# Four small edits to start, hand-over and tail of a layer-norm, sliding-window attention and gated-FFN kernel on one TensorE-bound core

## The chip, the cores and the metric

The kernel runs on one core of a Trainium2 chip (the other cores are idle). The metric is the device time of one execution in microseconds (us). "Fast" is the undisturbed state of an execution; every run named here was in it, at a granted TensorE clock of 0.999 or 1.0. Engines: PE is TensorE's matmuls, PEld its weight loads, DVE VectorE, ACT ScalarE, POOL GpSimd, SP SyncE, which here only issues DMAs. A trailing q (SPq) is an engine's queue of issues.

## The reference, cut to what matters

```python
x  = A_x                                   # 1 x 2048 x 640, bf16
xn = layernorm(x)                          # over the 640 columns
s  = attention(xn, k_cache, v_cache, wq, wo)   # 32 heads of 192, the last 512 cached keys
g  = silu( (silu(xn @ w_gate) * (xn @ w_up)) @ w_down )   # hidden width 1536
out = x + s * g
```

There are 16 row tiles of 128 rows, in four blocks of 512. The kernel first normalises the rows and does the whole FFN block by block, then scans over 16 pairs of heads times four blocks (64 "steps") for the attention, and last forms the output tiles.

## The kernel before

Four places matter. **The start.** x comes in row tiles; gate and up weights come in two pieces each, input chunks 0 and 1 first, then chunks 2 to 4 (the "late" weights):

```python
load_x(0, nc.scalar); load_x(1, nc.scalar)
load_first(slice(0, 2))        # gate, then up: chunks 0, 1
load_first(slice(2, NC))       # gate, then up: chunks 2, 3, 4
...
load_x(2); load_x(3)
...
banks = [(f, s) for f in range(3) for s in range(2)]      # s: 0 gate, 1 up
for t in range(4):                                        # row tiles of block 0
    order = [(*fs, [c]) for c in range(NC) for fs in banks]      # 30 matmuls
    if t == 3: order = [(*fs, range(NC)) for fs in banks]
    for k, (f, s, cs) in enumerate(order):
        if k == len(order) * 4 // 5 and t < 3:            # after 24 of the 30
            ...
            ln_apply(t + 1); ready(t + 1)      # normalise; TensorE transposes, copies to xnT
            ...
        hidden_mm(first[f][s][:, rows], s, f, rows, cs)
```

(At t = 1 the statistics of tile 3 are begun before the normalising pass of tile 2.) **The hand-over to the next block.** Rows of the following block are normalised by VectorE and transposed by DMA while a block's twelve hidden chunks f run:

```python
if nx and 6 <= f < 10:
    ln_apply(4 * b + f - 2)
    ln_transpose_dma(4 * b + f - 2)
```

**The first steps of the scan.** After the products with V, the contexts are divided by their row sums, on VectorE (`by_dve`) or on ScalarE. For steps 0 and 1 the first pair of row tiles accumulates in an `mm` tile of PSUM, the second in an `sc` tile; there are two tiles of each kind, so the next user of the tile waits for the division.

```python
st["acc"] = sc_tile() if i < 2 and q2 else mm_tile()
...
divide(i, q2, acc, (0, 1) if i < 2 and q2 == 0 else ())
```

**The tail.** Eight output tiles are written through a ring of four buffers, each of which is free again when its store has landed:

```python
ob = finp.tile([P, D], bf, name="ob", bufs=4)
...
V.tensor_tensor(to, ps, like(g2[:, t, cols]), ALU.mult)
eng.tensor_tensor(like(ob[:, cols]), to, like(sacc[:, t, cols]), ALU.add)   # eng: VectorE or GpSimd
```

The softmax here doesn't subtract the row's maximum and nothing guards it: scores larger than these inputs give would overflow.

Of the kernel before, what the change touches and what calls it, by code (L numbers as in the profile page):

```python
# [15 lines left out]
def kernel(  # L16
# [14 lines left out]
    P = nc.NUM_PARTITIONS  # L31
# [3 lines left out]
    Sq, D = x2.shape  # L35
# [7 lines left out]
    NC = D // P  # L43
# [10 lines left out]
    bf = dt.bfloat16  # L54
# [111 lines left out]
    with ExitStack() as fctx:  # L166
# [14 lines left out]
        def load_x(t, eng=nc.sync):  # L181
            x_t[t] = lnx.tile([P, D], bf, name="x_t")
            eng.dma_start(out=x_t[t][:], in_=x2[t * P : (t + 1) * P, :])
# [65 lines left out]
        def ln_sqrt(t):  # L249
            mv, rstd = ln[0]  # L250
            nc.scalar.activation(
                rstd[:, t : t + 1], mv[:, t, 1:2], ACT.Sqrt, bias=eps_t[:], scale=1.0
            )

        def ln_apply(t, parts=(slice(0, D),)):
            b, ti = divmod(t, 4)
            mv, rstd = ln[b]
            xns[t] = lnx.tile([P, D], bf, name="xn", bufs=4)
            if b == 0:
                nc.vector.reciprocal(rstd[:, t : t + 1], rstd[:, t : t + 1])  # L260
            for cols in parts:
                nc.vector.tensor_scalar(
                    xns[t][:, cols], x_t[t][:, cols], mv[:, ti, 0:1], rstd[:, ti : ti + 1],
                    op0=ALU.subtract, op1=ALU.mult,
                )

        def ln_transpose_dma(t):
            nc.sync.dma_start_transpose(
                out=xnT[:, 0:NC, t * P : (t + 1) * P], in_=xns.pop(t)[:]
            )  # L270
# [69 lines left out]
        for t in range(4):  # L340
            rows = slice(t * P, (t + 1) * P)

            order = [(*fs, [c]) for c in range(NC) for fs in banks]
            if t == 3:
                order = [(*fs, range(NC)) for fs in banks]
            for k, (f, s, cs) in enumerate(order):
                if k == len(order) * 4 // 5 and t < 3:
                    if t == 1:
                        ln_stats(3, lambda: ln_apply(2))
                    else:  # L350
                        ln_apply(t + 1)
                    ready(t + 1)
                    if t == 0:
                        ln_stats(2)
                    if t < 2:
                        ln_sqrt(t + 2)
                    else:
                        nc.scalar.activation(act_t[:], one_t[:], ACT.Silu)
                hidden_mm(first[f][s][:, rows], s, f, rows, cs)
                if t == 3 and s == 1:  # L360
                    hidden_gate(0, f, *first[f])
# [5 lines left out]
        for b in range(NB):  # L367
            if b:
                hTs[b] = ffh.tile([P, NF, 512], bf, name="hT")
            nx = b + 1 < NB  # L370
            u = 0
            for f in range(NF):
                if nx and b and f == 0:
                    for t in range(4 * b + 4, 4 * b + 8):
                        load_x(t)
                if b or f >= 4:
                    ffn_hidden(b, f)
                if nx and 2 <= f < 6:
                    ln_stats(4 * b + 2 + f)
                    if f == 5:  # L380
                        ln_rstd(b + 1, 0, 4)
                if nx and 6 <= f < 10:
                    ln_apply(4 * b + f - 2)
                    ln_transpose_dma(4 * b + f - 2)

                if b >= 1 and f % 3:
                    ffn_down(b - 1, u)
                    u += 1
                if b == 2:
                    if f == 0:  # L390
                        load_k(0)
                    elif 2 <= f < 6:
                        transpose_k(0, f - 2)
                    elif f == 6:
                        load_wq(0)
                    elif 7 <= f < 10:
                        sum_k(0, f - 7)
                elif b == 3:
                    if f < 5:
                        centre_k(0, f)  # L400
                    elif f < 8:
                        (load_k, load_wq, load_wo)[f - 5]((1, 1, 0)[f - 5])
# [12 lines left out]
    finp = ctx.enter_context(tc.tile_pool(name="fin", bufs=2))  # L415
# [5 lines left out]
    Ps, OTs, Obs, xrs = {}, {}, {}, {}  # L421
# [34 lines left out]
    def pv(i, q2):  # L456

        pr, b = divmod(i, NB)
        st = {}

        def part(p):
            if p == 0:
                if q2 == 0:
                    Obs[i] = opool.tile([P, 4, 2, Dh], bf, name="O_b")
                    tag = "OT_l" if late(i) and pr < last else "OT_b"
                    OTs[i] = otpool.tile([P, 12, P], bf, name=tag, tag=tag, bufs=2 if tag == "OT_l" else 3)
                st["acc"] = sc_tile() if i < 2 and q2 else mm_tile()
            acc = st["acc"]
            turn, h = divmod(p, 2)
            for kc in range(KC):  # L470
                for n, r in enumerate((lo, hi)):
                    k = n ^ turn
                    qt = 2 * q2 + k
                    m = nc.tensor.matmul(  # L474
                        acc[:, k, h * 256 : h * 256 + Dh + 1],
                        Ps[i][kc][r, h, qt * P : (qt + 1) * P], V_p[r, kc, h, 0 : Dh + 1],
                        start=(p == 0 and kc == 0), stop=(turn == 1 and kc == KC - 1),
                        skip_group_check=True,
                    )
                    after(m, st)  # L480
            if p == 1:
                turned(m, st)
            if p == 3:
                divide(i, q2, acc, (0, 1) if i < 2 and q2 == 0 else ())

        return [lambda p=p: part(p) for p in range(4)]

    def divide(i, q2, acc, by_dve):
        pr, b = divmod(i, NB)
        O_b, OT_b = Obs[i], OTs[i]  # L490
        r = smpool.tile([P, 2, 2, 1], f32, name="r")
        a_v = acc[:, :, :].rearrange("p k (h c) -> p k h c", h=2)
        nc.vector.reciprocal(r[:], a_v[:, :, :, Dh : Dh + 1])  # L493
        for k in range(2):
            qt = 2 * q2 + k
            a_k = a_v[:, k, :, :]
            if by_dve and k in by_dve:
                nc.vector.tensor_tensor(
                    O_b[:, qt, :, :], a_k[:, :, 0:Dh], r[:, k, :, :].to_broadcast([P, 2, Dh]),
                    ALU.mult,  # L500
                )
                continue
            for h in range(2):
                nc.scalar.activation(  # L504
                    O_b[:, qt, h, :], a_k[:, h, 0:Dh], ACT.Copy, scale=r[:, k, h, :]
                )
        nc.sync.dma_start_transpose(
            out=OT_b[:, 6 * q2 : 6 * q2 + 6, :],
            in_=O_b[:, 2 * q2 : 2 * q2 + 2, :, :].rearrange("p t h d -> p (t h d)"),
        )  # L510
# [121 lines left out]

    def wo_last(b, qt, eng):
        i, t = last * NB + b, 4 * b + qt
        ob = xrs[t] if b < 2 else finp.tile([P, D], bf, name="ob", bufs=4)
        s_f = finp.tile([P, D], f32, name="s_f", bufs=4)
        sc = mm_tile() if b == 2 and qt % 2 == 0 else sc_tile()
        for n, cols in enumerate(HALVES):
            if late(i):
                wo_cols(sc[:, n, 0:HD], i - NB, qt, cols, end=False)  # L640
            wo_cols(sc[:, n, 0:HD], i, qt, cols, first=not late(i))
        finish(sc[:, :, 0:HD], t, slice(0, D), ob, s_f, eng)
        stores.append((t, ob))

    def wo_parts(qt, parts):


        i, t, c0 = NS - 1, 4 * (NB - 1) + qt, 0
        ob = finp.tile([P, D], bf, name="ob", bufs=4)
        s_f = finp.tile([P, D], f32, name="s_f", bufs=4)  # L650
        for n, (width, eng, queue) in enumerate(parts):
            cols, c0 = slice(c0, c0 + width), c0 + width
            ps = (sc_tile() if n else mm_tile())[:, 0, 0:width]
            wo_cols(ps, i - NB, qt, cols, end=False)
            wo_cols(ps, i, qt, cols, first=False)
            finish(ps, t, cols, ob, s_f, eng)
            if queue:
                queue.dma_start(out=out2[t * P : (t + 1) * P, cols], in_=ob[:, cols])
        if not queue:
            stores.append((t, ob))  # L660
# [25 lines left out]
    for pr in range(NPAIR):  # L686
        for b in range(NB):
            i = pr * NB + b
# [22 lines left out]
        for b in range(NB):  # L711
            i = pr * NB + b
# [17 lines left out]
    i = last * NB  # L730
# [47 lines left out]
```

## Time and profile before

| | kernel before |
|---|---|
| time, the first three runs | 922.9 us median (922.84 to 922.93) |
| span of the profiled execution | 921.8 us (timed at 923.55 us, 0.65 above that median) |
| TensorE / VectorE / ScalarE / GpSimd busy | 914.4 / 576.0 / 474.0 / 101.5 us |
| first matmul starts / last one ends | 1.23 / 917.83 us |

The page of the profile cuts the span into 40 slices of 23 us; a digit is the busy share in tenths.

```profile
PE   8999999999999999999999999999999999999998
DVE  6443331467676767676666667676767676767656
ACT  4222223547464656555556565655555555556461
```

TensorE is at 9 in every slice but the first and the last: no other engine can be the bound, and whatever the change can win lies in the first slice, in the last, and in stalls too short to change a digit. That is why one has to go to the timeline.

### The profile page before, as it was taken

The numbers are of one execution on the slowest core, as the hardware profiler recorded it, in microseconds if no ns is written. First come the engines' busy times: TensorE is split into PE (matmuls) and PEld (weight loads), VectorE is DVE, ScalarE is ACT, GpSimd is POOL, SyncE is SP. The second block draws the span as 40 slices with busy tenths as digits, with TensorE's granted clock in tenths as the row PEclk, the third lists the DMA queues.
The fourth block names the chain that finished last, engine by engine and source line by source line (L and its number), as shares of the span: only waits on it lengthen the run. The fifth ranks groups of instructions, "written<-read, shape, count | busy, mean of one in ns | idle before, by whom it ended". The sixth has DMA issues, their size and how long they took to land.

```text
span 921.8 us, 25768 instructions
## 1 busy us (share of the span) xinstructions
PE 914.4 (99%) x11086; PEld 625.7 (68%) x11102; DVE 576.0 (62%) x847; ACT 474.0 (51%) x850; POOL 101.5 (11%) x390
## 2 busy tenths in 40 slices
PE   8999999999999999999999999999999999999998
PEld 5455555575858585868686767676777777776666
DVE  6443331467676767676666667676767676767656
ACT  4222223547464656555556565655555555556461
POOL 0000000000000000000000000000000000002978
PEclk9999999999999999999999999999999999999999
DMA  9312510044544444444536262635271817163524
GB/s 309 62 22 70 101 45 1 1 74 92 91 76 83 83 81 86 73 93 63 103 58 108 56 112 53 113 47 120 43 123 36 130 37 129 29 128 86 134 58 141
DMA packets 243762, 77.18 MB, mean 84 GB/s; under 512 B 224576, under 2 KB 243648, under 8 KB 243648
## 3 DMA queue, kind: packets, MB, share of 16 engines
q1 hardware_dynamic: 243216, 75.14, 41.6%
q8 instruction: 87, 1.43, 0.7%
q10 hardware_dynamic: 432, 0.39, 0.2%
q14 instruction: 27, 0.22, 0.1%
HBM read 39.45 MB, written 2.62 MB: 46 GB/s over the span
## 4 chain that ended last, share of the span: by engine, by line
PE 98%; DMA 1%; POOL 0%; DVE 0%; issue 0%; SPq 0%; POOLq 0%; DVEq 0%
PE mm L435 22%; PE sc L571 19%; PE sc L449 18%; PE mm L474 16%; PE sc L277 11%; PE mm L299 6%; PE sc L543 2%; PE mm L526 2%; DMA wu_sb<-in_B_w_up_dram 1%; PE gu L277 0%; DMA out_dram<-ob 0%; PE mm L543 0%; PE mm L312 0%; PE sc L474 0%; PE sc L526 0%; POOL ob L631 0%
## 5 line engine op out<-in xcount | busy, mean ns | idle before, releaser
L453 ACT ACTIVATE p_t<-sc 128x1024 bf16<-128x1024 f32 x254 | 252.9, 1022 | 128.4 <-PE sc L449 128.4
L440 DVE TENSOR_REDUCE qT<-mm 128x512 bf16<-128x1024 f32 x189 | 231.1, 1223 | 95.2 <-PE mm L435 92.8
L504 ACT ACTIVATE O_b<-mm,r 128x192 bf16<-128x192 f32 x482 | 163.2, 421 | 178.8 <-issue 156.3
L435 PE MATMUL mm<-xnT,wq_p 64*128 64x512 bf16 x1890 | 240.2, 376 | 0.0
L596 DVE TENSOR_TENSOR sacc<-sacc,sc 128x640 f32<-128x640 f32 x200 | 164.2, 821 | 86.8 <-PE sc L571 86.8
L571 PE MATMUL sc<-wo_p,OT_b 64*128 64x320 bf16 x2592 | 217.4, 296 | 0.0
L449 PE MATMUL sc<-qT,khat 64*128 64x512 bf16 x1524 | 198.2, 376 | 0.0
L474 PE MATMUL mm<-V_p,p_t 64*128 64x193 bf16 x3520 | 186.4, 242 | 0.0
L474 PEld LDWEIGHTS <-p_t 64*128 64x128 bf16 x3584 | 162.9, 93 | 12.0
L435 PEld LDWEIGHTS <-wq_p 64*128 64x128 bf16 x1890 | 105.7, 94 | 93.4 <-issue 0.5
L571 PEld LDWEIGHTS <-OT_b 64*128 64x128 bf16 x2592 | 140.4, 94 | 21.6 <-issue 0.2
L449 PEld LDWEIGHTS <-khat 64*128 64x128 bf16 x1536 | 85.9, 94 | 79.8
L559 POOL MEMSET turn_t<- 128x1 f32 x328 | 32.2, 98 | 692.3 <-PE mm L474 469.7
L285 DVE TENSOR_TENSOR hT<-sc,sg 128x512 bf16<-128x512 f32 x46 | 31.7, 691 | 84.0 <-ACT sg L284 84.0
L284 ACT ACTIVATE sg<-sc 128x512 bf16<-128x512 f32 x46 | 27.3, 596 | 73.7 <-PE sc L277 73.7
L277 PE MATMUL sc<-xnT,wu_sb 128*128 128x512 bf16 (+1 forms) x259 | 60.5, 354 | 0.5 <-DMA wu_sb<-in_B_w_up_dram 0.4
L277 PE MATMUL sc<-xnT,wg_sb 128*128 128x512 bf16 (+1 forms) x248 | 60.0, 353 | 0.9
L299 PE MATMUL mm<-wd_sb,hT 128*128 128x320 bf16 x384 | 56.6, 299 | 0.0
L493 DVE RECIPROCAL r<-mm 128x4 f32<-128x4 f32 x124 | 22.7, 183 | 47.1 <-PE mm L474 36.3
L299 PEld LDWEIGHTS <-hT 128*128 128x128 bf16 x384 | 37.6, 98 | 18.9
L277 PEld LDWEIGHTS <-wu_sb 128*128 128x128 bf16 x285 | 27.3, 98 | 27.5 <-DMA wu_sb<-in_B_w_up_dram 0.6
L277 PEld LDWEIGHTS <-wg_sb 128*128 128x128 bf16 x285 | 27.3, 98 | 23.1 <-issue 0.6
(69 smaller groups left out, 376.2 us busy)
## 6 DMA issues: line engine op xcount, KB each, us to landing
wo_p<-in_A_wo_dram SPq DMA_DIRECT2D x16, 480.0 KB, 4.3
K_p<-in_A_k_cache_dram SPq DMA_DIRECT2D x32, 192.0 KB, 3.3
V_p<-in_A_v_cache_dram SPq DMA_DIRECT2D x32, 192.0 KB, 3.1
wq_p<-in_A_wq_dram SPq DMA_DIRECT2D x64, 80.0 KB, 3.0
wq_p<-in_A_wq_dram SPq DMA_DIRECT2D x16, 160.0 KB, 3.6
x_r<-in_A_x_dram SPq DMA_DIRECT2D x16, 160.0 KB, 3.6
x_t<-in_A_x_dram SPq DMA_DIRECT2D x14, 160.0 KB, 3.1
OT_b<-O_b SPq DMA_TRANSPOSE x124, 2.9
```

The source lines that it names most:

```text
L277: nc.tensor.matmul(out, w_sb[:, c, f * P : (f + 1) * P], xnT[:, c, qc], start=(c == 0), stop=(c == NC - 1),)
L285: nc.vector.tensor_tensor(hTs[b][:, f, :], u, sg[:], ALU.mult)
L299: nc.tensor.matmul(dn[:, 0:HD], hTs[b][:, f, ti * P : (ti + 1) * P], wd_sb[:, f, cols], start=(f == 0), stop=(f == NF - 1),)
L435: nc.tensor.matmul(q_ps[:, h, :], pairs[pr]["wq"][r, c, j * P : (j + 1) * P], xnT[r, c, b * 512 : (b + 1) * 512], start=(c == 0), stop=(c ...
L440: nc.vector.reduce_sum(qTs[i][:, j, :], q_ps[:, :, :].rearrange("p h n -> p n h"), axis=AX.X)
L449: nc.tensor.matmul(sc[:, h, :], khat[r, j, ks], qT[r, j, :], start=(j == 0), stop=(j == 2))
L453: nc.scalar.activation(p_t[:, :, :], sc[:, :, :], ACT.Exp, scale=scale)
L474: m = nc.tensor.matmul(acc[:, k, h * 256 : h * 256 + Dh + 1], Ps[i][kc][r, h, qt * P : (qt + 1) * P], V_p[r, kc, h, 0 : Dh + 1], start=(p ...
L504: nc.scalar.activation(O_b[:, qt, h, :], a_k[:, h, 0:Dh], ACT.Copy, scale=r[:, k, h, :])
L559: st["turn"] = nc.gpsimd.memset(turn_t[:], 0.0)
L571: m = nc.tensor.matmul(ps[:, n, 0:HD], OTs[i][r, 3 * qt + j, :], pairs[i // NB]["wo"][r, j, n * HD : (n + 1) * HD], start=(turn == 0 and j ...
L596: nc.vector.tensor_tensor(s_t, s_t, sc[:, :, 0:HD], ALU.add)
```

## The change

The intent: each edit removes one short stall of TensorE or of the tail. In row tile 0 the matmuls on the late up weights, which land last, go behind those on the late gate weights. The next block's rows are normalised two per chunk, so that their DMA transposes are done sooner. In step 1 the two divisions swap engines. And the output ring gets six buffers.

```diff
             order = [(*fs, [c]) for c in range(NC) for fs in banks]
-            if t == 3:
+            if t == 0:
+                order = order[:12] + [
+                    (f, s, [c]) for s in range(2) for c in range(2, NC) for f in range(3)
+                ]
+            elif t == 3:
                 order = [(*fs, range(NC)) for fs in banks]
...
-                if nx and 6 <= f < 10:
-                    ln_apply(4 * b + f - 2)
-                    ln_transpose_dma(4 * b + f - 2)
+                if nx and f in (6, 7):
+                    for t in range(4 * b + 2 * f - 8, 4 * b + 2 * f - 6):
+                        ln_apply(t)
+                        ln_transpose_dma(t)
...
-                divide(i, q2, acc, (0, 1) if i < 2 and q2 == 0 else ())
+                divide(i, q2, acc, (0, 1) if q2 == i else ())
...   (in both places that take an output buffer)
-        ob = finp.tile([P, D], bf, name="ob", bufs=4)
+        ob = finp.tile([P, D], bf, name="ob", bufs=6)
```

More of the change, by code (lines that the diff above doesn't have):

```diff
@@ L634, in wo_last @@
         i, t = last * NB + b, 4 * b + qt
-        ob = xrs[t] if b < 2 else finp.tile([P, D], bf, name="ob", bufs=4)
+        ob = xrs[t] if b < 2 else finp.tile([P, D], bf, name="ob", bufs=6)
         s_f = finp.tile([P, D], f32, name="s_f", bufs=4)
```

## The prediction

> **What bounds the kernel now.** I read first the busy shares, then the chain of work that ended last, then the list of who waited for whom, and then the timeline at the four places that the change touches.
>
> ```profile
> PE 914.4 (99%) x11086; PEld 625.7 (68%) x11102; DVE 576.0 (62%) x847; ACT 474.0 (51%) x850; POOL 101.5 (11%) x390
> ...
> PE 98%; DMA 1%; POOL 0%; DVE 0%; issue 0%; SPq 0%; POOLq 0%; DVEq 0%
> ```
>
> TensorE is busy for 914.4 of 921.8 us, and 98% of the closing chain is TensorE. The change adds and removes no matmul, so all that can shrink is the 7.4 us in which TensorE is not busy, together with short stalls that the modelled matmul ends cover. About 4 us of those 7.4 is the tail after the last matmul, 1.2 us is the start, 0.7 us the wait for the first normalised tile; little is in reach. The listed waits of TensorE are only these three:
>
> ```profile
> PE gu L225 <- DVE zero_t L174: 1.2, 1, 1.2
> PE tp L326 <- DVE xn L262: 0.7, 1, 0.7
> PE sc L277 <- DMA wu_sb<-in_B_w_up_dram: 0.4, 1, 0.4
> ```
>
> So I price each part by what it takes off one stall, and ask whether the next wait takes it back.
>
> **What the Trainium skill says.** "Perfetto Trace Analysis", Identifying the Most-Contended Engine, says that busy time of matmuls does not tell how close a kernel is to its ceiling, because matmuls are pipelined. The trace agrees in one way that matters here: a matmul shown as 219 ns follows its neighbour by 55 ns (7.05, 7.10, 7.16 in the timeline), so a stall can hide in the shown lengths and I take stalls from the starts. "DMA: Bandwidth & Descriptors", Anatomy of one DMA, puts a fixed cost of about 2 us on each DMA, most of it until the written bytes are confirmed (stated for the GpSimd path); the stores here land 1.9 us after issue (median, SyncE queue), but one took 4.0 us. "Perfetto Trace Analysis", Optimizing Tensor Performance, wants independent matmul groups to rotate through PSUM banks so that evacuation overlaps; part 3 is about two such accumulators whose evacuation comes just too late.
>
> **Part 1: row tile 0 takes the late up chunks last.** Tile 0 has 30 matmuls: twelve on input chunks 0 and 1, then eighteen on chunks 2 to 4. Their late gate and up weights are separate transfers, and up lands last.
>
> ```profile
> 7.16 0.22 PE L277 MATMUL sc<-xnT,wg_sb 128*128 128x128 bf16 x1
> 7.79 0.23 PE L277 MATMUL sc<-xnT,wu_sb 128*128 128x128 bf16 x1 [0.41 <-DMA wu_sb<-in_B_w_up_dram]
> ```
>
> The first late gate matmul runs at 7.16; the up matmul behind it would start at 7.22 and starts at 7.79, a loss of 0.57 us by starts. The new order puts nine gate matmuls first: 9 x 0.055 = 0.5 us, so the first up comes at 7.66 and still waits about 0.13 us for 7.79. TensorE is then 0.44 us (8 x 0.055) ahead. Does that last? The next tile but one needs its normalised rows for the transposes of line 326, and these come from a chain that TensorE does not feed:
>
> ```profile
> 8.23 0.89 DVE L238 BATCH_NORM_STATS2 stats<-x_t 128x6 f32<-128x320 bf16 x2 [0.46 <-DMA x_t<-in_A_x_dram]
> ...
> 9.92 0.45 DVE L262 TENSOR_SCALAR xn<-x_t,mv,rstd 128x640 bf16<-128x640 bf16 x1
> ...
> 10.44 0.32 PEld L326 LDWEIGHTS <-xn 128*128 128x128 bf16 x5
> ```
>
> VectorE waits for the load of row tile 2 until 8.23, then statistics, square root, reciprocal and the normalising pass end at 9.92 + 0.45 = 10.37. Earlier handovers from this pass to the transpose's weight load took 0.05 us (5.69 to 5.74, 5.98 to 6.03), so tile 2 cannot be loaded before 10.42; it is loaded at 10.44 now. TensorE would reach that point at about 10.0 and wait 0.4 us there. So the listed wait for the up weights shrinks or vanishes and a new wait of the transposes on the normalised rows takes its place. **Gain: 0.02 us.**
>
> **Part 2: two row tiles normalised per chunk.** Block 0 normalises and transposes one tile of block 1 after each of hidden chunks 6 to 9; the change does two after chunk 6 and two after 7. In the timeline the fourth pass runs at 31.56, its DMA transpose is issued at 32.02 and lands 2.6 us later, at 34.6. Block 1 begins there:
>
> ```profile
> 32.28 1.24 PE L277 MATMUL sc<-xnT,wg_sb 128*128 128x512 bf16 x5
> 33.36 1.24 PE L277 MATMUL sc<-xnT,wu_sb 128*128 128x512 bf16 x5
> 34.73 1.24 PE L277 MATMUL sc<-xnT,wg_sb 128*128 128x512 bf16 x5
> 35.80 1.24 PE L277 MATMUL sc<-xnT,wu_sb 128*128 128x512 bf16 x5
> ```
>
> Groups start 1.08 us apart, except here: 34.73 - 33.36 = 1.37, so 0.29 us is lost, though no list of waits names it. The weight loads show it too (0.59 us idle at 34.70, where 0.11 to 0.13 is usual). With the change, the passes of 0.45 us start at about 25.5, 26.0, 27.2 and 27.7. One transpose holds the SyncE queue 1.2 us, so they are issued near 26.0, 27.2, 28.4 and 29.6; with the slowest landing of the case, 3.9 us, the last is there at 33.5, before 34.44, when TensorE wants it. Cost: VectorE has two passes in a row, 0.9 us, behind one hidden product; the next product waits for ScalarE until 2.15 us after the last and itself takes 0.69, which leaves 2.15 - 0.61 = 1.5 us. It fits. Later blocks show no such gap (starts 1.08 or 1.63 us apart around 73.66 and 112.60), so they gain nothing. **Gain: 0.29 us.**
>
> **Part 3: the second step's two divisions swap engines.** Only step 1 changes; step 0 keeps its division and later steps have none on VectorE. Today the accumulator of the first row pair (in mm) is divided by VectorE (1.02 us), the other (in sc) by ScalarE (four activations, 1.35 us), whose reciprocal must wait for VectorE:
>
> ```profile
> 197.41 1.02 DVE L498 TENSOR_TENSOR O_b<-mm,r 128x384 bf16<-128x384 f32 x2
> 198.35 0.17 DVE L493 RECIPROCAL r<-sc 128x4 f32<-128x4 f32 x1
> 198.56 1.35 ACT L504 ACTIVATE O_b<-sc,r 128x192 bf16<-128x192 f32 x4 [2.40 <-DVE r L493]
> ...
> 199.40 1.15 PE L571 MATMUL sc<-wo_p,OT_b 64*128 64x320 bf16 x12
> ```
>
> The sc tile comes free at 199.91. The twelve output matmuls from 199.40 occupy 0.97 us until the next group starts at 200.37, against 0.81 for the same twelve later (201.04 to 201.85): the second half waited 0.16 us for that tile. Swapped, the reciprocal of the sc pair runs near 197.87 and VectorE ends near 199.1, so this wait goes. But ScalarE now divides the mm pair: it starts 0.21 to 0.27 us after the reciprocal's start at 197.19, ends 1.35 later at 198.75 to 198.81, and the tile reaches TensorE about 0.05 us after. Its next user is the group that starts at 198.73. That is a new wait of about 0.1 us where there were 0.3 us of slack. **Gain: 0.16 - 0.10, about 0.05 us.**
>
> **Part 4: six output buffers instead of four.** In the closing chain:
>
> ```profile
> 912.26 4.02 DMA out_dram<-ob
> ...
> 916.40 0.49 DVE ob L631
> ...
> 917.43 0.85 POOL ob L631
> ```
>
> The seventh output tile reuses the third one's buffer, whose store is issued at 912.26 and lands at 916.28. VectorE, done multiplying at 915.93, can add only at 916.40: 0.47 us idle. Freed, the addition runs at 915.95 and the second half's multiplication at 916.33 (its matmuls end at 915.63 + 0.57 = 916.20). GpSimd starts that half at about 917.0 instead of 917.42 and ends 0.86 us later, at 917.8. The last tile's multiplication, bound by matmuls ending at 916.53 + 0.65 = 917.18, goes only from 917.29 to 917.22 and ends at 917.78, so GpSimd starts the last addition at 917.9 instead of 918.24, and the last SyncE store goes from 919.26 to about 918.9. The other closing store, issued at 918.80, stays: its matmuls end at 917.83 either way. **Gain: 0.34 us**, if that slow landing is there without the profiler; were it a usual 1.9 us, the buffer would have been free at 914.2 and the gain nil. I count 0.25.
>
> **Sum.** 0.02 + 0.29 + 0.05 + 0.25 = 0.61 us: 922.9 - 0.6 = 922.3 us.
>
> **The rivals.** (a) Part 1 keeps its 0.44 us, because row tile 2 arrives early enough. Its load would have to land sooner, and nothing in the change moves it; against it speaks the 0.46 us for which VectorE waits at 8.23. It would make 921.9. (b) Part 4 is worth nothing since the 4.0 us landing belongs to the profiled execution, and part 3 turns its wait into an equal one: 922.6. For it: the other early stores land in 1.9 us. (c) VectorE becomes the bound where two normalising passes stand in a row and the sc tiles come free late: this would cost up to 0.9 us in each of three blocks, up to 925. Against it are the 1.5 us of room above. (d) The transposes are hidden anyway and part 2 gives nothing: 922.6; against it, the 0.29 us gap sits at the one place that needs the fourth transpose.
>
> **Range and chances.** All parts holding in full with (a) make 921.8; only part 2, less a few hundredths lost in part 3, makes 922.65. The three runs of before spread over 0.09 us, so the range is the uncertainty of the parts plus about 0.1 us for changed placement: 921.75 to 922.8. Two per cent is 18.5 us, more than twice all time in which TensorE is not busy; faster by that is out of reach, slower would need a recurrent stall in the scan, whose code is untouched. Hence 0.005, 0.99 and 0.005.
>
> **What would show it right or wrong.** In the changed profile: the wait on the up weights near 0.1 us and a new one of the transposes on the normalised rows near 10 us, with tile 2 loaded at 10.4 still; the start of block 1 at 34.4, 1.08 us after the group before; the group of step 2 near 198.5 about 0.1 us late, and the twelve output matmuls back at 0.81 us; no idle time of VectorE before the seventh tile's addition. Wrong if tile 2's weights load at 10.0, if block 1 still starts with a gap, or if the tail from the last matmul to the end is not shorter by about 0.3 us.

## The result, and the profile after

The changed kernel took 922.75 us median (922.36 to 923.64, six runs), the kernel before 923.34 (922.84 to 924.70, six runs). The ratio is 0.9993, with a 95% interval from 0.998 to 1.0006: the same within 2%, and not told apart from 1 either. (A ratio is the mean time of one kernel's fast runs over the mean of the fast runs of the kernel before that are listed with it, so it is not quite the ratio of the medians.) The runs of one kernel spread over more than a microsecond, so what follows is read from the traces, place by place, and timing only bounds it.

The profiled execution of the changed kernel is 1.1 us shorter, 920.7 us. First its page:

```profile
PE 914.6 (99%) x11086; PEld 625.9 (68%) x11102; DVE 575.8 (63%) x847; ACT 474.6 (52%) x850; POOL 101.9 (11%) x390
...
PE 98%; POOL 0%; DMA 0%; DVE 0%; issue 0%; POOLq 0%; ACT 0%; DVEq 0%
```

Work and bound are as before, and DMA has left the second place of the closing chain. Next, all that the list of waits has of TensorE (us in total, times, longest):

```profile
PE gu L225 <- DVE zero_t L174: 1.2, 1, 1.2
PE tp L326 <- DVE xn L262: 0.2, 1, 0.2
```

The wait on the up weights is gone; no new wait on normalised rows beside the first tile's is listed. The timeline shows row tile 2 (statistics, normalising pass, weights of the transposes):

```profile
7.72 0.88 DVE L238 BATCH_NORM_STATS2 stats<-x_t 128x6 f32<-128x320 bf16 x2
...
9.40 0.45 DVE L262 TENSOR_SCALAR xn<-x_t,mv,rstd 128x640 bf16<-128x640 bf16 x1
...
9.90 0.31 PEld L326 LDWEIGHTS <-xn 128*128 128x128 bf16 x5
```

Tile 2 is loaded at 9.90 where it was 10.44: 0.54 us sooner, though the prediction gave this part 0.02. But the statistics, too, begin 0.51 us sooner, and without a wait for the load. Whether the new order did that is the first question for the experiments. Then the start of block 1, and step 1 with its successor:

```profile
31.74 1.24 PE L277 MATMUL sc<-xnT,wg_sb 128*128 128x512 bf16 x5
32.82 1.24 PE L277 MATMUL sc<-xnT,wu_sb 128*128 128x512 bf16 x5
33.90 1.24 PE L277 MATMUL sc<-xnT,wg_sb 128*128 128x512 bf16 x5
```

```profile
196.59 1.36 ACT L509 ACTIVATE O_b<-mm,r 128x192 bf16<-128x192 f32 x4 [1.25 <-DVE r L498]
...
197.25 1.02 DVE L503 TENSOR_TENSOR O_b<-sc,r 128x384 bf16<-128x384 f32 x2
...
197.50 0.57 PE L576 MATMUL sc<-wo_p,OT_b 64*128 64x320 bf16 x6
197.99 0.84 PE L479 MATMUL mm<-V_p,p_t 64*128 64x193 bf16 x16
198.66 0.99 PE L576 MATMUL sc<-wo_p,OT_b 64*128 64x320 bf16 x12
199.47 0.85 PE L479 MATMUL mm<-V_p,p_t 64*128 64x193 bf16 x16
```

Block 1 now starts 1.08 us after the group before it (1.37 before): 0.29 us won. In the second fence the twelve output matmuls occupy 199.47 - 198.66 = 0.81 us (0.97 before), but the group at 197.99 starts 0.49 us after the six before it, where it was 0.41 (198.32 to 198.73): ScalarE frees that accumulator only at 197.95. Net gain: 0.16 - 0.08 = 0.08 us. Last the tail, on VectorE, GpSimd and the closing stores' queues:

```profile
914.53 0.50 DVE L635 TENSOR_TENSOR mm<-mm,g 128x320 f32<-128x320 f32 x1 [0.33 <-PE mm L548]
915.06 0.49 DVE L636 TENSOR_TENSOR ob<-mm,sacc 128x320 bf16<-128x320 f32 x1
...
916.03 1.99 POOL L636 TENSOR_TENSOR ob<-s_f,sacc 128x320 bf16<-128x320 f32 x2 [0.60 <-DVE s_f L635]
...
917.90 0.35 ACTq L663 DMA_DIRECT2D out_dram<-ob  x1
918.04 0.33 SPq L663 DMA_DIRECT2D out_dram<-ob  x1
```

The addition follows the multiplication at once (0.47 us idle before). The last matmul ends at 916.94 and the last SyncE store goes out 1.10 us later; before it was 919.26 - 917.83 = 1.43. From that store to the end of the span it is 2.66 us, 2.54 before, so about 0.2 of these 0.33 us reach the end. The sum is 0.54 + 0.29 + 0.08 + 0.2 = 1.1 us, the difference of the spans; the cause of the 0.54 is open at this point.

### The profile page after: what moved, and what is told of

Its sections match the earlier page's. It is cut to its first block, busy times and chain, and to the rows that moved or that the text cites. A ratio compares the mean times of both kernels' runs of the same rounds, so it can differ in the third digit from the quotient of the medians.

```text
span 920.7 us, 25767 instructions
## 1 busy us (share of the span) xinstructions
PE 914.6 (99%) x11086; PEld 625.9 (68%) x11102; DVE 575.8 (63%) x847; ACT 474.6 (52%) x850; POOL 101.9 (11%) x390
## 3 DMA queue, kind: packets, MB, share of 16 engines
q8 instruction: 87, 1.43, 0.7%
## 4 chain that ended last, share of the span: by engine, by line
PE 98%; POOL 0%; DMA 0%; DVE 0%; issue 0%; POOLq 0%; ACT 0%; DVEq 0%
PE mm L440 22%; PE sc L576 19%; PE sc L454 18%; PE mm L479 16%; PE sc L277 11%; PE mm L299 6%; PE sc L548 2%; PE mm L531 2%; POOL ob L636 0%; PE gu L277 0%; PE mm L548 0%; PE mm L312 0%; DMA x_t<-in_A_x_dram 0%; PE sc L479 0%; PE sc L531 0%
```

## The experiments

All outputs are right. The two theories of the first question: **A**, the first loads land earlier or later from execution to execution, and the changed kernel's profile met an early one; **B**, the new order of part 1 brings them in. The kernels of a group ran one after another on one chip and share their runs of the kernel before.

**1 to 4. Both kernels again, part 1 alone, and the other three parts alone.** For the two repeats nothing is edited; `order_only` has the first hunk of the diff, `no_order` all the others.

> The kernel before, unchanged, with a new profile. In its first profile row tile 2 landed so late that VectorE began its statistics at 8.23 us and TensorE loaded the transposes of tile 2 at 10.44; in the profile of the changed kernel those were 7.72 and 9.90. Theory A (the landing of the first loads differs from execution to execution, and is not made by the change): the statistics of tile 2 begin anywhere between 7.7 and 8.3 here, the stall on the late up weights moves with it, and the five runs spread over 0.5 to 1.5 us. Theory B (the new matmul order itself brings the loads in earlier): statistics again at 8.2, transposes of tile 2 again at 10.4. Either way: 0.29 us gap before block 1, 0.16 us in the second step, 0.47 us idle before the seventh output tile's addition if the 4 us store is the rule, none if it was an accident. Time ratio 1.000.

> Part 1 alone. Theory A: tile 2's transposes start at whichever is later, TensorE's own arrival (about 10.0) or 2.2 us after the statistics of tile 2 begin; so 9.9 with an early landing and 10.4 with a late one, and the part is worth 0 to 0.5 us against the old order at the same landing. Theory B: 9.9 again whatever the landing. The gaps of the three other parts (0.29, 0.16 and, if it is the rule, 0.47 us) are all still there. Time ratio 0.9995 to 1.000.

> Parts 2, 3 and 4 without part 1. Block 1 starts 1.08 us after the group before it (0.29 us gained); second step gains about 0.08 (a new 0.08 us delay before the group that reuses the accumulator, the 0.16 us one gone); the last store goes out about 1.1 us after the last matmul instead of 1.4. The up weights stall is back (0.6 us by starts if they land at 7.7). Theory A: tile 2's transposes at the later of TensorE's arrival and 2.2 us after its statistics begin. Time ratio 0.9993 to 0.9997.

> The changed kernel, unchanged, with a new profile. Theory A: if row tile 2 lands late here (statistics after 8.0), the transposes of tile 2 start later than 10.1 and TensorE shows a new wait on the normalised rows. Theory B: 9.9 again. Parts 2 to 4 as in its first profile: block 1 without a gap, 0.08 us delay in the second step, no idle time before the seventh output tile's addition. Time ratio 0.9992 to 0.9995.

| | median us (range), 5 runs | ratio to before (95%) | profiled span |
|---|---|---|---|
| before_again | 923.83 (923.01 to 924.57) | 1.0006 (0.9993 to 1.0018) | 922.0 |
| order_only | 923.04 (922.75 to 923.65) | 0.9998 (0.9984 to 1.0012) | 921.9 |
| no_order | 923.07 (922.43 to 923.69) | 0.9998 (0.9986 to 1.0011) | 921.9 |
| after_again | 922.82 (922.51 to 923.67) | 0.9998 (0.9985 to 1.0010) | 920.7 |

Timing separates none of them. The traces do. Part 1 alone met a late landing; this is its timeline, and its waits of TensorE on normalised rows:

```profile
7.90 0.17 PEld L277 LDWEIGHTS <-wu_sb 128*128 128x128 bf16 x3 [0.30 <-DMA wu_sb<-in_B_w_up_dram]
...
8.33 0.89 DVE L238 BATCH_NORM_STATS2 stats<-x_t 128x6 f32<-128x320 bf16 x2 [0.62 <-DMA x_t<-in_A_x_dram]
...
10.52 0.28 PEld L326 LDWEIGHTS <-xn 128*128 128x128 bf16 x5 [0.38 <-DVE xn L262]
```

```profile
PE tp L326 <- DVE xn L262: 0.7, 2, 0.5
```

This is what the prediction drew: the stall on the up weights shrinks, VectorE still waits for row tile 2, and TensorE pays at 10.52 with a new wait for the normalised rows (two such waits where the kernel before had one). The saving is gone 2.6 us after the up weights landed (7.90 to 10.52). Theory B has lost its simple form, for here the new order is in and the landing is late. The gap before block 1 is 1.37 us in `before_again` and `order_only` (33.65 to 35.02, 33.40 to 34.77), and 1.08 in `no_order` and `after_again`; the group in step 2 comes 0.41 us after its six and the twelve matmuls take 0.97 to 0.98 in the first two, 0.50 and 0.81 to 0.82 in the last two. Parts 2 and 3 have their size whatever the start did. (They were not run apart from each other; they are told apart by their places, near 34 and 198 us.)

**5 and 6. Take away what limits: row tile 2 first.** In both, the load of tile 2 goes ahead of the late weights; the second also has the new order.

```diff
         load_first(slice(0, 2))
+        load_x(2)
         load_first(slice(2, NC))
-        load_x(2)
         load_x(3)
```

> The kernel before with the load of row tile 2 moved ahead of the late gate and up weights, so that tile 2 no longer limits: a baseline for the next run. Up weights land about 0.45 us later than in the kernel before, so the stall in row tile 0 grows to about 1 us by starts; the statistics of tile 2 start near 7.7 us without waiting for the load, and the transposes of tile 2 follow TensorE's own arrival, about 2.65 us after the first late up matmul, near 10.9 (10.4 with an early landing).

> The same with the new order of part 1. If the saving of part 1 is real and is taken back only by row tile 2's late landing, it stays here: the first up matmul follows nine gate matmuls at the landing of the up weights, and the transposes of tile 2 start about 2.2 us after the first late up matmul instead of 2.65, that is 0.44 us sooner for the same landing, with no wait on the normalised rows. If the order gains nothing even so, the distance stays near 2.65 us or a wait on the normalised rows appears.

Old order first, then new, from the first late up weights to the transposes of tile 2:

```profile
9.25 0.10 PEld L277 LDWEIGHTS <-wu_sb 128*128 128x128 bf16 x1 [0.79 <-DMA wu_sb<-in_B_w_up_dram]
...
11.90 0.32 PEld L326 LDWEIGHTS <-xn 128*128 128x128 bf16 x5
```

```profile
8.82 0.17 PEld L277 LDWEIGHTS <-wu_sb 128*128 128x128 bf16 x3 [0.40 <-DMA wu_sb<-in_B_w_up_dram]
...
11.03 0.32 PEld L326 LDWEIGHTS <-xn 128*128 128x128 bf16 x5
```

The distance is 2.65 us with the old order and 2.21 with the new: 0.44 us saved and kept, with no wait on normalised rows in either. So the saving of part 1 is real, and it is row tile 2 that takes it back. As a version this is no good: the late weights themselves land later, and the medians were 923.76 us (923.21 to 924.89, four runs) and 923.14 (922.98 to 923.97, four runs), ratios 1.0001 (0.9987 to 1.0016) and 0.9993 (0.9977 to 1.0008).

**7 and 8. An attempt at a better version, and two more landings.** Both pairs of step 1 are shared by both engines; `split` is that on the changed kernel, `split_old` the same without part 1.

```diff
-                divide(i, q2, acc, (0, 1) if q2 == i else ())
+                divide(i, q2, acc, (0, 1) if i == q2 == 0 else (0,) if i == 1 else ())
```

> The changed kernel, with the second step's two divisions each shared by both engines (VectorE the first row tile of a pair, ScalarE the second). Both accumulators should be free before they are wanted: the group after the first six output matmuls starts 0.41 us after them (0.49 to 0.50 in the changed kernel, 0.41 before) and the twelve output matmuls occupy 0.81 us (0.97 before). Gain 0.08 us against the changed kernel, too small for the timing: ratio against the kernel before 0.9990 to 0.9998. It is also a third sample of the loads' landing with the new order: early (7.7) or late (8.2 to 8.6) statistics of row tile 2.

> The same without part 1 (old order in row tile 0): another sample of the landing with the old order. If the landing is early, the up weights should be there near 7.2 us and the old order should stall little (under 0.2 us), with the transposes of tile 2 near 9.9 as with the new order: then part 1 is worth nothing in either case. If part 1 is what brings the loads in early (theory B), the landing is late here again and in the run before it is early. Second step as in the run before it.

The edit misses its aim. The timeline of `split` around the division of the mm pair:

```profile
196.61 0.18 DVE L498 RECIPROCAL r<-mm 128x4 f32<-128x4 f32 x1 [0.78 <-PE mm L479]
196.83 0.56 DVE L503 TENSOR_TENSOR O_b<-mm,r 128x384 bf16<-128x384 f32 x1
...
197.48 0.73 ACT L509 ACTIVATE O_b<-mm,r 128x192 bf16<-128x192 f32 x2 [1.90 <-DVE r L498]
...
197.74 0.57 PE L576 MATMUL sc<-wo_p,OT_b 64*128 64x320 bf16 x6
198.26 0.84 PE L479 MATMUL mm<-V_p,p_t 64*128 64x193 bf16 x16
```

ScalarE does not start beside VectorE, 0.21 us after the reciprocal's start, but only when VectorE's half is done (196.83 + 0.56 = 197.39). The two halves run one after the other, and the group starts 0.52 us after its six (0.41 hoped for, 0.49 in the changed kernel). Which dependency orders them was not tested. The list of waits of the kernel before has the same pattern where other divisions are shared, and could have warned:

```profile
ACT O_b L504 <- DVE O_b L498: 2.2, 3, 1.2
```

The medians, 922.57 us (922.51 to 922.76) and 922.45 (922.38 to 922.79), with ratios 0.9987 (0.9975 to 1.0) and 0.9986 (0.9974 to 0.9999), are the lowest and steadiest so far. The edit can't be why, since it costs 0.03 us where it acts; both profiles met an early landing. In `split_old`, with the old order, tile 2's statistics begin at 7.76, so the landing can be early without part 1.

**9 to 12. The landing once more, in reversed order, and part 4 alone.** `after_third` and `before_third` are the two kernels unchanged, `order_only_2` is part 1 alone again, `bufs_only` has only the last hunk of the diff.

> The changed kernel again, this time first of its group; before_third, the kernel before, is last. In the two groups of runs so far the first loads landed late in the profiles taken first and early in those taken last, whatever the kernel. Theory A (the landing is not made by the kernel): the landing here may be late (statistics of row tile 2 at 8.2 us or later), and then the transposes of tile 2 start 2.2 us after them with a wait on the normalised rows, at 10.4 or later. Theory B (this kernel makes the loads land early): statistics at 7.7 to 8.0 and transposes at 9.9 to 10.2, as in both its profiles so far.

> Part 1 alone, a second profile. With a late landing: transposes of tile 2 2.2 us after its statistics begin, as in the first profile (2.19). With an early one: 3.36 to 3.40 us after the first matmul's weights of tile 0, against 3.62 for the old order. Time ratio 0.999 to 1.000.

> Part 4 alone. Last SyncE store issued 1.1 us after the modelled end of the last matmul whether the third output store lands in 2 or in 4 us; with four buffers it was 1.42 to 1.49 when it took 4 us and 1.10 when it took 1.9. Gaps of parts 2 and 3 are back: 1.37 us before block 1, 0.97 us for the twelve output matmuls. Old order in row tile 0. Time ratio 0.9995 to 1.000.

> The kernel before, last of its group. Theory A: the landing may be early here; then statistics of tile 2 begin before 8.0 us and the transposes of tile 2 start about 3.6 us after the first weights of tile 0, near 10.2. Theory B: late again, at 8.2 to 8.5, transposes at 10.4 to 10.7. Tail: 1.42 us to the last store if the third store takes 4 us, 1.1 if it takes 2. Time ratio 1.000.

Medians and ratios: `after_third` 922.52 us (922.42 to 922.80), 0.9992 (0.9978 to 1.0006); `order_only_2` 923.02 (922.75 to 923.19), 0.9996 (0.9984 to 1.0009); `bufs_only` 922.94 (922.85 to 924.18), 0.9999 (0.9987 to 1.0012); `before_third` 923.21 (922.77 to 924.17), 1.0000 (0.9987 to 1.0012). The idea that the place in the group decides the landing fell: the first was early, the last later than any. `before_third` shows what a late landing does, here with both late weights overdue:

```profile
PE sc L277 <- DMA wu_sb<-in_B_w_up_dram: 0.7, 1, 0.7
PE sc L277 <- DMA wg_sb<-in_B_w_gate_dram: 0.4, 1, 0.4
```

Here are all the profiles with the original order of loads (us; "distance" is from the statistics of tile 2 to its transposes):

| profile | order | tile 2: statistics | transposes loaded | distance |
|---|---|---|---|---|
| before | old | 8.23, waited for the load | 10.44 | 2.21 |
| before_again | old | 8.51, waited | 10.72 | 2.21 |
| no_order | old | 8.63, waited | 10.84 | 2.21 |
| before_third | old | 9.05, waited | 11.27 | 2.22 |
| order_only | new | 8.33, waited | 10.52 | 2.19 |
| split_old | old | 7.76 | 10.19 | 2.43 |
| bufs_only | old | 7.76 | 9.94 | 2.18 |
| after | new | 7.72 | 9.90 | 2.18 |
| after_again | new | 7.77 | 9.95 | 2.18 |
| after_third | new | 7.64 | 9.88 | 2.24 |
| order_only_2 | new | 7.68 | 9.87 | 2.19 |
| split | new | 7.97 | 10.15 | 2.18 |

The statistics begin anywhere from 7.64 to 9.05, and the transposes follow 2.18 to 2.24 us later with either order, but for one profile. Part 1 is worth 2.21 - 2.19 = 0.02 us when the landing is late and nothing when it is early (`bufs_only`, 2.18, against the new order's 2.18). The exception, `split_old`, is not a matter of the order. Its tile 1 transposes come only at 8.11 (7.90 in `bufs_only`), so ScalarE is still at its copies (8.48 to 9.23) when tile 2's variance is ready (8.89), begins the square root at 9.12, and VectorE waits 0.21 us for it. But that delay begins with the first six matmuls of tile 0, which both orders share; the up weights cost nothing:

```profile
6.62 0.31 PE L277 MATMUL sc<-xnT,wu_sb 128*128 128x128 bf16 x1
6.73 0.31 PE L277 MATMUL sc<-xnT,wg_sb 128*128 128x128 bf16 x1
...
7.50 0.22 PE L277 MATMUL sc<-xnT,wg_sb 128*128 128x128 bf16 x1
7.55 0.22 PE L277 MATMUL sc<-xnT,wu_sb 128*128 128x128 bf16 x1
```

Five of these first steps are 0.11 us here and 0.055 in `bufs_only`, which makes tile 0's seventh matmul 0.26 us late (7.16 against 6.90, both kernels having begun at 6.57); why they were slow was not found. The late up weights (7.55 above) follow the late gate weights by 0.05 us, without a wait. `bufs_only` has no such wait either, so an early landing leaves the new order nothing to save, and the vanished wait in the changed kernel's first profile does not speak for part 1.

Can the order have made the landing? The kept traces settle it. In all twelve profiles the loads are issued at the same times: the late gate weights at 1.74 us, the late up weights at 2.24 or 2.25, row tile 2 at 2.77 or 2.78. Only the time from issue to landing (the last number, us) differs; here it is for the late weights in `bufs_only` and then in `before_third`, both in the old order:

```profile
wg_sb<-in_B_w_gate_dram SPq DMA_DIRECT2D x1, 288.0 KB, 4.3
wu_sb<-in_B_w_up_dram SPq DMA_DIRECT2D x1, 288.0 KB, 4.7
...
wg_sb<-in_B_w_gate_dram SPq DMA_DIRECT2D x1, 288.0 KB, 5.9
wu_sb<-in_B_w_up_dram SPq DMA_DIRECT2D x1, 288.0 KB, 6.3
```

The gate weights took 4.2 to 4.7 us in the seven early profiles and 5.1 to 5.9 in the five late ones, so they had landed by 6.5 us or not before 6.8. The two orders first differ at the fourteenth matmul of tile 0, which comes no sooner than 7.1 us in any of the twelve. The executions have thus parted before the order can act: theory B falls, and 0.54 us of the difference of the first two spans was the landing. What sets the landing stays open, and with it why the changed kernel was early in all three of its profiles and the kernel before late in all three. Row tile 2 landed 0.45 to 0.73 us after the up weights in all twelve, so late up weights come with a late tile 2.

Part 4 shows in the tail of every profile. "Tail" is from the modelled end of the last matmul to the issue of the last SyncE store.

| buffers | third store took | tail | profiles |
|---|---|---|---|
| 4 | 4.0 to 4.1 us | 1.42 to 1.49 us | before, before_again, order_only |
| 4 | 1.9 to 2.0 us | 1.10 to 1.11 us | order_only_2, before_third, x2_first_old, x2_first_new |
| 6 | 3.7 to 4.1 us | 1.10 to 1.11 us | after, after_third, no_order, bufs_only, split, split_old |
| 6 | 2.0 us | 1.11 us | after_again |

Part 4 alone (`bufs_only`), with a slow third store, has the addition right behind the multiplication:

```profile
914.91 0.50 DVE L630 TENSOR_TENSOR mm<-mm,g 128x320 f32<-128x320 f32 x1 [0.32 <-PE mm L543]
915.44 0.49 DVE L631 TENSOR_TENSOR ob<-mm,sacc 128x320 bf16<-128x320 f32 x1
```

`order_only_2`, with four buffers and a quick store, has only 0.09 us between them and the same short tail:

```profile
914.85 0.50 DVE L634 TENSOR_TENSOR mm<-mm,g 128x320 f32<-128x320 f32 x1 [0.32 <-PE mm L547]
915.44 0.49 DVE L635 TENSOR_TENSOR ob<-mm,sacc 128x320 bf16<-128x320 f32 x1
```

So two more buffers win nothing when the store is quick and about 0.3 us of tail when it is slow, which it was in 9 of 14 profiles. Only part of that reaches the end: from the last matmul to the end of the span it is 3.9 to 4.0 us in the first row of the table and 3.7 to 3.8 in the others, 0.2 less, because the last SyncE store itself landed 1.6 us after its issue in the first row and 1.7 in the others. (The "third store" is the third one from the ring of buffers.)

## Why the prediction was right

**The bound.** TensorE stays at 99% with the same matmuls, and 922.75 us lies in the range of 921.75 to 922.8, near its upper end. It sits high because in those rounds the kernel before, too, was above the 922.9 us that the prediction started from: the difference of the medians, 923.34 - 922.75 = 0.59 us, is the 0.6 that was summed. Part of that match is luck: one kernel's runs spread over more than a microsecond, and the gains were read from an execution of 923.55 us but taken off the 922.9 us of quicker ones. All 16 runs of the changed kernel have a median of 922.69 us, all 43 of the kernel before 923.19: 0.5 us, pooled over chips. The parts as measured below sum to 0.02 + 0.29 + 0.08 + 0.13 = 0.52 us.

**Part 1, 0.02 us: right in mechanism, with one premise wrong.** The new wait on the normalised rows came where it was drawn, with `order_only` at 10.52, and the late-landing distances give 0.02 us. Experiments 5 and 6 show the other half, that the 0.44 us are real where tile 2 doesn't limit. Wrong was the step that took the landing at 8.23 as fixed: tile 2 landed at 7.3 to 9.0 us in different executions of the same loads. So the sign that the prediction set for its own failure, tile 2 loaded at 10.0, came true (9.90) without the reason behind it failing. It should have been a distance, 2.2 us from the statistics, and not a clock time. Rival (a), that the saving is kept because tile 2 comes early, had its condition met but not its gain: an early tile 2 comes with early up weights, for which the old order did not wait either (`bufs_only`, `split_old`).

**Part 2, 0.29 us: exact.** 1.36 to 1.37 us became 1.08 in every profile that has it. One step of the working was too quick: the third transpose held SyncE's queue for 1.8 us, not 1.2, so the fourth was issued at 30.12 us (30.66 on the clock of the profile before, where 29.6 was written). It landed at 32.76, still 1.1 us before block 1 wanted it. Rivals (c) and (d) fell: no new wait for VectorE shows, and the transposes were not hidden.

**Part 3, 0.05 us: 0.08 measured.** The wait removed was 0.16 us as read; the new one was put at 0.10 and is 0.08 to 0.09.

**Part 4, 0.34 us when the store is slow, counted as 0.25.** The last store moved by 0.33 us, as worked out; about 0.2 reach the end of the span. The step that took the issue of that store for the end was wrong by its landing, 1.7 us where it had been 1.6, so the prediction's third sign of failure (a tail to the end not shorter by about 0.3) came true by half. Discounting for a store that may be quick was right in kind: it is no accident of one execution, nor the rule. Weighed by the 9 of 14 profiles, 0.2 us is worth 0.13 (an estimate), half of the 0.25 that was counted. Half of rival (b) is true whenever the store is quick.

## What to carry to other kernels

When one engine is at 99%, price an edit by the stall it removes and then follow that engine to its next hand-over: if what it needs there comes from a chain that the edit doesn't touch, the stall only moves. Look for stalls in the distances between starts as well as in the list of waits (the largest sure gain, 0.29 us, is in no list), and state what would refute a prediction as a distance between two events rather than as a clock time. Below 0.1% of the span, repeated timing with a spread of a microsecond can't rank versions; take the traces' local distances from several executions.

## What the Trainium skill lacked or had wrong

- "DMA: Bandwidth & Descriptors", Anatomy of one DMA, gives the fixed cost of about 2 us as nearly constant (for the GpSimd path; further on, the page lets it grow with HBM load, which no run here varied). Stores of 160 KB from SyncE's queue landed in 1.8 to 2.1 us mostly, but the third one from the ring of buffers took 3.7 to 4.1 us in 9 of 14 profiles (and the two after it 2.1 to 2.9), against 1.9 to 2.0 in the other five. What delays it was not found.
- No page that was consulted says how far the same first loads of a kernel may land apart from one execution to the next: with the same loads issued at the same times, row tile 2 took 4.5 to 6.3 us from issue to landing.
- "Perfetto Trace Analysis", Identifying the Most-Contended Engine, says that pipelined TensorE instructions look smaller in a trace. Here, where the ends are modelled, they look longer than their spacing: 219 ns shown, 55 ns from start to start, and the 0.29 us stall before block 1 is in no list of waits.
